# PSUM as one tile of eight single banks: a gated mix of an S4D convolution and a ReLU feed-forward

## The chip, the cores and the metric

The kernel runs on one core of one Trainium2 chip. Its time is the device time of one execution in microseconds; lower is better. The time before is the median of three runs. A profile is one execution of its own, and its span goes from the first to the last instruction.

## The reference

Everything is fp32. With `u` of 2048 positions by 640 channels (N = 128 states, a hidden width of 1728), shortened:

```python
g  = sigmoid((u * gate_w).sum(-1, keepdims=True))
dt = exp(log_dt); A = -exp(log_A_real) + 1j*A_imag; C = (C_real + 1j*C_imag) * dt[:, None]
K  = 2 * einsum("dn,dnl->dl", C, exp((A*dt[:, None])[:, :, None] * pos)).real   # 640 x 2048
a  = causal_conv(K, u) + u * D_skip          # through an FFT of length 4096 in the reference
b  = relu(u @ w1) @ w2
out = g * a + (1 - g) * b
```

## The kernel before

Three kinds of work share the engines.

*Feed-forward.* Each fp32 operand is split into a high and a low fp32r part, and a product is three matmuls (high-high, high-low, low-high). The 1728 hidden columns are 14 blocks, worked off in three passes (`PARTS`, 5, 5 and 4 blocks), each over all eight groups of 256 positions. `hidden` and `wide` make the hidden layer, `sums` multiplies by w2; the sum of a pass goes through DRAM to the next. ScalarE (ACT) makes the high part from PSUM, VectorE (DVE) the low part. All its accumulators are the PSUM tile `pf`, a pool of two single banks.

*Generation of K* (`products`, `factors`, `taps`): TensorE (PE) makes phases and exponents into a four-bank tile `pg`, ACT takes exp and sin, DVE multiplies, and PE sums over the states into `pk` (one bank, also used to transpose `u`). K goes to DRAM (`kd`). Together with `pe` (one bank) these three fill the other six banks until K is done.

*Convolution* (`conv`), in five tiles of 128 channels, as a transform in two stages, a complex product, and the same back. A tile's buffer is `ku`, two of which exist. Its steps, with the names of their task queues:

- stage 1 (`sk` for K, `su` for u): four tasks each, a 64-point transform by the table `tf`; DVE transposes the result in blocks of 32 by 32 from PSUM into `ku`, two instructions a task. `load_u` fetches u for one tile into `xu`.
- stage 2 (`s2`): eight groups j; PE multiplies by `tm`. PSUM then holds the transforms of K and of u. ACT copies that of K to `ku`, DVE makes the two kinds of products into `ku` and `kx`, GpSimd (POOL) adds and subtracts.
- inverse stage 2 (`inv2`, table `tn`), halves h = 0 and 1, each needing the POOL results of its four groups; ACT copies back to `ku`.
- relay (`rl`): eight DVE transposes; then inverse stage 1 (`inv1`, queue `s4`, table `tw`), ACT multiplies by the gate, POOL adds the feed-forward's part sum, and the result leaves through SyncE (SP) queues.

All PSUM of the convolution is the tile `pc`, a pool of three, each of two banks. Every step there works on both banks at once: one ACT copy reads 512 elements a partition from two half banks, and a u transpose reads 16 columns of both.

The order of all work is written out: each piece is a task in a queue, and a string `ORDER` (one letter a task, a number before it repeats) says which queue's next task is issued. This sets each engine's own order, and engines then wait for each other by semaphores alone. PE's queue mixes feed-forward blocks between those of the other two kinds. All instructions are recorded through one helper, so a row of the profile has the helper's line, L186 (L185 in the changed kernel), and tiles tell the steps apart.

A row of PE's order counts an fp32 matmul once, while the profile records it twice: the order's `tm ... x16` (one group of stage 2) is the profile's x32. Feed-forward matmuls are fp32r and are recorded once.

Of the kernel before, what the change touches and what calls it, by code (L numbers as in the profile page):

```python
# [26 lines left out]
LATE = 4  # L27
KX = 3
# [7 lines left out]
YJ = 2  # L36
# [83 lines left out]
class Token:  # L120


    def __init__(self, ring):
        self.ring, self.left = ring, 0


class Ring:
    def __init__(self, n):
        self.free = n
# [6 lines left out]
class Plan:  # L136
# [25 lines left out]
    def run(self):  # L162
        queues = {k: iter(self.queues.pop(tuple(x.split('.')))) for k, x in QUEUES.items()}
        assert not self.queues, list(self.queues)
        for n, k in re.findall(r'(\d*)(\D)', ORDER):
            for _ in range(int(n or 1)):
                t = next(queues[k])
                assert all(d.done for d in t.deps), (k, n)
                for b in t.take:
                    b.ring.free -= 1  # L170
                    assert b.ring.free >= 0, (k, n)
                t.fn()
                t.done = True
                for b in (*t.take, *t.use):
                    b.left -= 1
                    b.ring.free += b.left == 0
# [30 lines left out]
class Kernel:  # L207
    def __init__(self, tc, ctx, io, out):
# [20 lines left out]
        self.pb = ctx.enter_context(tc.tile_pool(name="psf", bufs=2, space=PSUM))  # L229
# [7 lines left out]
    def feed_forward(self):  # L237
# [3 lines left out]
        pa, pb = self.pa, self.pb  # L241
        for n, k in dict(ws=3, wq=5, wo=2, xs=XS, xhl=2, q=2, bank=2, z=1).items():
            ring(n, k)
# [92 lines left out]
        def trans(g, third, src):  # L336
            s_, ld = src
            bank = ('pk', 'pe', 'pg')[0 if g else third]
            b_ = tok(bank)
# [5 lines left out]
            def pe():  # L345
                ps = self.psg.tile([128, 8 if bank == 'pg' else 2, 256], F32, name=bank)
                ps = st['xb', g, third] = ps[:, :2]
# [13 lines left out]
            a = A('PE', 'ff', pe, [ld], take=[b_], use=[s_])  # L361
# [31 lines left out]
        def hidden(p, g, i, fs):  # L393
            b_, h_ = tok('bank'), tok(f"h{i}")

            def pe(r, f, third):
                def go():
                    if r == third == 0:
                        st['hb'] = st['hb', i] = pb.tile([128, 2, 256], F32, name="pf")
# [56 lines left out]
        def wide(p, P, f):  # L456
            ring_ = ("h0", "h2")[f] if f < 2 else f"hw{f}" if p == 1 else ("w14", "w24")[f - 2]
            b_, h_, xs_ = tok('bank'), tok(ring_), [xtok[p, 2 * P + i] for i in range(2)]
# [37 lines left out]
        def sums(p, g, j, q_, qld):  # L496
# [8 lines left out]
            b_ = tok('bank')  # L505
# [7 lines left out]
            def pe(ks):  # L513
                def go():
                    if ks[0] == 0:
                        st['sb', g, j] = pb.tile([128, 320], F32, name="pf")
# [85 lines left out]
        def spin():  # L602
            p = self.psg.tile([128, 2, 256], F32, name="pe").rearrange("p a b -> p (a b)")
            for _ in range(SPIN):
                self.E.matmul(p[:, :128], self.ident, self.ident, start=True, stop=True)
        if SPIN:
            A('PE', 'ff', spin)
# [3 lines left out]
        def spread_gate():  # L611
            p = st['gb'] = self.psg.tile([128, 8, 256], F32, name="pg").rearrange("p a b -> p (a b)")[:, :D]
# [99 lines left out]
        self.last_wide = done[1, 1],  # L712
        for x, gs in self.need_sums:
# [140 lines left out]
    def ssm(self, C=16):  # L854
# [8 lines left out]
        self.c_ps, self.psg = self.cm_enter(name="psg", bufs=1, space=PSUM)  # L863
# [492 lines left out]
```

## Time and profile before

| | us |
|---|---|
| runs | 620.28, 621.45, 622.0; median 621.45 |
| profiled execution | 621.33 |
| its span | 619.5 (1.8 less than its own time) |
| PE busy | 605.9 (98%) |
| DVE busy | 505.9 (82%) |
| ACT busy | 376.1 (61%) |
| POOL busy | 83.9 (14%) |

Rows read: engine, operation, output tile, input tiles, shapes, count; then busy time and the mean of one in ns; then the engine's idle time ahead of them and what ended it. In a timeline a row is start, length, and the merged instructions, with an idle time in brackets. The matmuls overlap in the array, so a length is longer than the step from one start to the next; it is the steps between starts that add up to time.

### The profile page before, as it was taken

The page shows a single profiled execution, that of the slowest core. Times are in us where ns is not written, and L with a number is a line of the kernel's source. Part 1 is how long each engine was busy: PE and PEld are TensorE (multiplying, and loading weights), DVE is VectorE, ACT ScalarE, POOL GpSimd, SP SyncE. Part 2 cuts the span into 40 slices and gives each one's busy share as a digit, 9 for nine tenths or more (in the row PEclk, how much of TensorE's full clock was granted, in tenths as well). Part 3 has the DMA queues.
Part 4 walks back from the last instruction along what each step waited for, and adds up shares of the span by engine and source line. Part 5 has one row for each costly group of instructions (what it writes and reads, how often), then busy time and mean ns, then how long its engine had stood idle before and what let it go on. Part 6 is the DMA issues. An engine that isn't in the chain of part 4 may idle for free.

```text
span 619.5 us, 19956 instructions
## 1 busy us (share of the span) xinstructions
PE 605.9 (98%) x8676; PEld 492.8 (80%) x8676; DVE 505.9 (82%) x841; ACT 376.1 (61%) x539; POOL 83.9 (14%) x114
## 2 busy tenths in 40 slices
PE   7999999999999999999999999999999999999997
PEld 6999998889987898898898888676646755667666
DVE  3798966899999999999999966887859768968642
ACT  3654438999999998899989821313351453432561
POOL 0000000000000000000000000024250360731735
PEclk8999999999999999999999999999999999999999
DMA  9783666135246535453643338982526766664276
GB/s 232 199 321 93 213 218 221 42 81 163 82 134 216 189 138 185 162 170 82 212 165 137 111 116 259 280 247 84 110 75 226 179 156 197 151 168 158 67 200 184
DMA packets 75457, 102.56 MB, mean 166 GB/s; under 512 B 7529, under 2 KB 58601, under 8 KB 75114
## 3 DMA queue, kind: packets, MB, share of 16 engines
q1 hardware_dynamic: 74970, 100.39, 53.8%
q8 instruction: 68, 1.11, 0.8%
q10 hardware_dynamic: 400, 0.90, 0.5%
q14 instruction: 19, 0.16, 0.1%
HBM read 62.21 MB, written 39.06 MB: 163 GB/s over the span
## 4 chain that ended last, share of the span: by engine, by line
PE 76%; ACT 8%; DVE 7%; DMA 4%; issue 2%; SPq 1%; POOL 1%; ACTq 0%; DVEq 0%; POOLq 0%
PE pf L186 51%; PE pc L186 15%; PE pk L186 6%; PE pg L186 4%; ACT sc L186 4%; DVE ku L186 3%; ACT L186 2%; SPq L186 1%; ACT mg L186 1%; DMA xu<-in_A_u_dram 1%; DMA ck<-kd 1%; DVE sc L186 1%; DVE mg L186 1%; DVE G L186 1%; DMA out_dram<-yo 1%
## 5 line engine op out<-in xcount | busy, mean ns | idle before, releaser
L186 PE MATMUL pf<-xx,w1h 128*128 128x256 f32 (+1 forms) x760 | 187.0, 344 | 0.0
L186 PEld LDWEIGHTS pf<-xx,w1h 128*128 128x128 f32 x760 | 124.9, 192 | 28.0 <-issue 13.4
L186 POOL TENSOR_TENSOR ku<-ku,kx 128x256 f32<-128x256 f32 x80 | 56.7, 738 | 473.5 <-DVE ku L186 438.3
L186 PE MATMUL pf<-xx,w1l 128*128 128x512 f32 (+1 forms) x340 | 115.9, 341 | 0.0
L186 ACT COPY ku<-pc 128x512 f32<-128x512 f32 (+1 forms) x60 | 43.7, 753 | 100.4 <-PE pc L186 89.1
L186 PE MATMUL pf<-w2h,hh 128*128 128x320 f32 x288 | 91.4, 322 | 0.3 <-DVE q L186 0.3
L186 DVE STREAM_TRANSPOSE ku<-pc 128x512 f32<-128x512 f32 x80 | 76.8, 1063 | 17.3 <-PE pc L186 17.3
L186 PE MATMUL pf<-w2l,hh 128*128 128x320 f32 x288 | 87.7, 308 | 0.0
L186 PE MATMUL pf<-w2h,hl 128*128 128x320 f32 x256 | 73.7, 313 | 0.0
L186 PEld LDWEIGHTS pf<-xx,w1l 128*128 128x128 f32 x340 | 64.9, 191 | 7.5
L186 PEld LDWEIGHTS pf<-w2h,hh 128*128 128x128 f32 x288 | 54.0, 188 | 11.1 <-issue 5.3
L186 ACT ACT_TABLE_LOAD x42 | 53.9, 1283 | 1.7 <-DVE sc L186 1.0
L186 PEld LDWEIGHTS pf<-w2l,hh 128*128 128x128 f32 x288 | 54.1, 188 | 0.2
L186 DVE TENSOR_TENSOR mg<-mg,sc 128x1024 f32<-128x1024 f32 x40 | 49.0, 1224 | 3.5 <-DVE G L186 0.5
L186 ACT COPY sc<-pg 128x1024 f32<-128x1024 f32 x40 | 40.4, 1010 | 14.7 <-PE pg L186 14.6
L186 DVE TENSOR_TENSOR sc<-sc,mg 128x1024 f32<-128x1024 f32 x40 | 48.6, 1216 | 0.0
L186 PEld LDWEIGHTS pf<-w2h,hl 128*128 128x128 f32 x256 | 46.4, 188 | 2.0 <-issue 1.2
L186 ACT ACTIVATE sc<-sc,half_pi 128x1024 f32<-128x1024 f32 x40 | 45.6, 1140 | 0.0
L186 ACT ACTIVATE hh<-pf 128x512 fp32r<-128x512 f32 (+1 forms) x40 | 20.4, 510 | 36.5 <-PE pf L186 36.5
L186 ACT ACTIVATE sc<-sc 128x1024 f32<-128x1024 f32 x40 | 42.2, 1054 | 0.2
L186 ACT ACTIVATE mg<-pg 128x1024 f32<-128x1024 f32 x40 | 41.7, 1043 | 0.2
L186 PE MATMUL pc<-ku,tm 64*32 64x256 f32 x1280 | 39.8, 379 | 0.6 <-DVE ku L186 0.5
(171 smaller groups left out, 1127.3 us busy)
## 6 DMA issues: line engine op xcount, KB each, us to landing
xx<-xt SPq DMA_DIRECT2D x24, 640.0 KB, 6.5
xt<-xx SPq DMA_DIRECT2D x16, 640.0 KB, 5.0
part<-q SPq DMA_DIRECT2D x16, 640.0 KB, 4.7
q<-part SPq DMA_DIRECT2D x16, 640.0 KB, 4.6
ws<-in_B_w_dram SPq DMA_DIRECT2D x20, 320.0 KB, 3.4
kd<-kt SPq DMA_DIRECT2D x80, 64.0 KB, 3.1
ck<-kd SPq DMA_DIRECT2D x40, 128.0 KB, 3.4
xu<-in_A_u_dram SPq DMA_DIRECT2D x10, 512.0 KB, 8.4
```

The source lines that it names most:

```text
L186: return lambda *a, **k: self._tc.keep_in_program_order(f(*a, **k))
```

## The change

One PSUM tile `ps` of 128 x 8 x 512 fp32 replaces the pools `pf`, `pg`, `pk`, `pe` and `pc`. A ring `bk` of eight hands out single banks, first freed first taken, to all three kinds of work. Four of the eight are held for `pg` (banks 0 to 3) until K is done, so that feed-forward, taps and input transposes share four in that time and everything shares eight afterwards.

In the convolution each instruction now touches one bank. Stage 1 and inverse stage 1 take two single banks, stage 2 two, inverse stage 2 four. `load_u` fetches halves of the channels: a partition half holds 32 positions by 64 channels (runs of 256 bytes in DRAM) where it held 16 by 128 (runs of 512 bytes), so that a transpose of u reads one bank. In stage 2 ACT makes two copies of 256 elements a group where it made one of 512; DVE still makes two products of 512 elements, but one a bank, both into `kx`; POOL takes both operands from `kx`. The ACT copies back after inverse stage 2 are four of 512 elements where there were two of 1024. `kx` has two buffers of twice the size where it had three. The part sums that are added at the end of a tile lie in `xu` behind u, in one buffer where there were two. Buffers of the convolution open later (`room`): after the last sums of the second pass, where they opened when K was done. And `ORDER` is another one throughout.

The numbers of matmuls, DVE products, transposes and POOL additions are the same; ACT has 60 copies more.

```diff
 class Ring:
     def __init__(self, n):
-        self.free = n
+        self.free = list(range(n))
...
                 for b in t.take:
-                    b.ring.free -= 1
-                    assert b.ring.free >= 0, (k, n)
+                    b.slot = b.ring.free.pop(0)
...
+        self.hold = [tok('bk') for _ in range(4)]
+        self.prm0 = A('PY', 'open', lambda: None, take=self.hold)
...
-        opened = self.opened = A('PY', 'open', start, [self.kd_out])
+        opened = A('PY', 'open', lambda: None, [self.kd_out], use=self.hold)
+        room = self.room = A('PY', 'open', start, [opened])
...
+        self.room.deps += done[1, 0].deps + done[1, 1].deps
...
-                    D_.dma_start(t[64 * h:64 * h + 64], ud[:, 16 * h:16 * h + 16, i * C:i * C + C])
+                    D_.dma_start(t[64 * h:64 * h + 64], ud[:, :, i * C + h * H:i * C + h * H + H])
...
         def stage2(i, j, dep):
-            b_, x_ = tok('psc'), tok('kx')
+            bs, x_ = [tok('bk') for _ in range(2)], tok('kx')
...
-                            self.E.matmul(ps[32 * m:32 * m + 32, p, 2 * a:2 * a + 2], st['tm'][r, g, 32 * a:32 * a + 32],
-                                          st['ku', i][r, :, g], start=True, stop=True)
+                            self.E.matmul(self.ps[32 * m:32 * m + 32, bs[p].slot, 256 * a:256 * a + 256],
+                                          st['tm'][r, g, 32 * a:32 * a + 32], st['ku', i][r, :, g], start=True, stop=True)
...
-            def copy():
-                S.copy(whole(i, j), st['p2', i, j][:, 0])
+            def copy(p):
+                return lambda: S.copy(halves(p), parts(p)[:, 0])
...
-                    V.tensor_mul(st['kx', i, j] if a else k, st['p2', i, j][:, 1, None, a].to_broadcast([128, 2, 2, C]), k)
+                    V.tensor_mul(st['kx', i, j][:, p], parts(p)[:, 1, :, None].to_broadcast([128, 2, 2, C]),
+                                 halves(p)[:, None].to_broadcast([128, 2, 2, C]))
...
-                    y, x = whole(i, j)[:, k], st['kx', i, j][:, 1 - k]
-                    (P.tensor_add if k else P.tensor_sub)(y, y, x)
+                    x = st['kx', i, j]
+                    (P.tensor_add if k else P.tensor_sub)(whole(i, j)[:, k], x[:, :, 0, k], x[:, :, 1, 1 - k])
...
-            bs = tok('psc'), tok('psc')
+            bs = [tok('bk') for _ in range(4)]
```

PE's order at the second tile's stage 2. `pf` are feed-forward matmuls; `pc<-ku,tm` is stage 2 (x16 is one group), `tw` inverse stage 1 of the tile before, `tn` half an inverse stage 2. Before:

```order
L186 MATMUL pc<-ku,tm 32x256 x48
L186 MATMUL pf<-xx,w1h_5364 128x512 x2
L186 MATMUL pf<-xx,w1l_5365 128x512
L186 MATMUL pc<-ku,tm 32x256 x16
L186 MATMUL pf<-xx,w1h_5364 128x512 x2
L186 MATMUL pf<-xx,w1l_5365 128x512
L186 MATMUL pc<-ku,tm 32x256 x32
L186 MATMUL pf<-xx,w1h_5364 128x512 x2
L186 MATMUL pf<-xx,w1l_5365 128x512
L186 MATMUL pc<-ku,tm 32x256 x32
L186 MATMUL pc<-ku,tw 64x512 x8
```

The same place in the changed kernel, from the end of the feed-forward stretch that parts the tile's two runs of four groups:

```order
L185 MATMUL ps<-xx,w1h_4974 128x512 x2
L185 MATMUL ps<-xx,w1l_4975 128x512
L185 MATMUL ps<-ku,tm 32x256 x64
L185 MATMUL ps<-ku,tw 64x512 x8
L185 MATMUL ps<-ku,tn 64x128 x64
L185 MATMUL ps<-ck,tf 64x512 x8
L185 MATMUL ps<-xx,w1h_5197 128x512 x2
```

Short feed-forward pieces between groups are gone; the eight groups are two runs of four, and the second is followed by three other steps of the convolution at once. Counted over all of PE's order from the first stage 1 on, feed-forward stands between convolution blocks in 26 places where it stood in 44, and the blocks of one kind of convolution matmul (`tf`, `tm`, `tn`, `tw`) number 49 where they numbered 58. Runs of up to five groups of stage 2 occur (twice).

DVE's order at the third tile's stage 2 (`ku<-ku` are relay transposes of the tile before, `ku<-pc` or `ku<-ps` with 128x16x32 the transposes of stage 1, `q` and `hl` feed-forward). Before:

```order
L186 SCALAR_TENSOR_TENSOR q<-pf,omg,q 128x320
L186 TENSOR_TENSOR kx<-pc,ku 128x512
L186 STREAM_TRANSPOSE ku<-ku 128x8x2x32 x2
L186 TENSOR_TENSOR ku<-pc,ku 128x512
L186 TENSOR_TENSOR kx<-pc,ku 128x512
L186 SCALAR_TENSOR_TENSOR q<-pf,omg,q 128x320
L186 TENSOR_TENSOR ku<-pc,ku 128x512
L186 STREAM_TRANSPOSE ku<-ku 128x8x2x32 x2
L186 TENSOR_TENSOR kx<-pc,ku 128x512
L186 STREAM_TRANSPOSE ku<-ku 128x8x2x32
L186 TENSOR_TENSOR ku<-pc,ku 128x512
```

In the changed kernel:

```order
L185 STREAM_TRANSPOSE ku<-ku 128x8x2x32
L185 TENSOR_TENSOR kx<-ps,ku 128x512 x6
L185 STREAM_TRANSPOSE ku<-ku 128x8x2x32 x2
L185 TENSOR_TENSOR kx<-ps,ku 128x512 x4
L185 SCALAR_TENSOR_TENSOR hl_6829<-ps,hh_6828 128x512
L185 TENSOR_TENSOR kx<-ps,ku 128x512 x6
L185 STREAM_TRANSPOSE ku<-ps 128x16x32 x16
```

Products of three groups (six), two and three stand together, where other work stood between nearly all of the first four.

PE's order at the very start (`ident` alone are warm-up matmuls, `ident,xu` the transposes of the first input, `gw,ones` the spread of the gate's weights). Before:

```order
L186 MATMUL pe<-ident 128x128 x10
L186 MATMUL pk<-ident,xu 128x128 x4
L186 MATMUL pe<-ident,xu 128x128 x4
L186 MATMUL pg<-ident,xu 128x128 x2
L186 MATMUL pg<-gw,ones 128x512
```

And now:

```order
L185 MATMUL ps<-ident 128x128 x10
L185 MATMUL ps<-ident,xu 128x128 x8
L185 MATMUL ps<-gw,ones 128x512
L185 MATMUL ps<-gw,ones 128x128
L185 MATMUL ps<-ident,xu 128x128 x2
```

The gate's matmul stands ahead of the last transposes and in banks of its own. On SP the first input now goes ahead of the first weights, which went first; on ACT the split of those first weights goes ahead of the splits of the input, which went first.

More of the change, by code (lines that the diff above doesn't have):

```diff
@@ L175, in run @@
                     b.left -= 1
-                    b.ring.free += b.left == 0
+                    if b.left == 0:
+                        b.ring.free.append(b.slot)
         assert not any(next(q, None) for q in queues.values())
@@ L337, in trans @@
             s_, ld = src
-            bank = ('pk', 'pe', 'pg')[0 if g else third]
-            b_ = tok(bank)
+            b_ = tok('bk')
             if third == 0:
@@ L345, in pe @@
             def pe():
-                ps = self.psg.tile([128, 8 if bank == 'pg' else 2, 256], F32, name=bank)
-                ps = st['xb', g, third] = ps[:, :2]
+                ps = st['xb', g, third] = self.ps[:, b_.slot].rearrange("p (k t) -> p k t", t=256)
                 for k in range(kn):
@@ L393, in hidden @@
         def hidden(p, g, i, fs):
-            b_, h_ = tok('bank'), tok(f"h{i}")
+            b_, h_ = tok('bk'), tok(f"h{i}")
             def pe(r, f, third):
@@ L601, in feed_forward, with spin @@
         self.zs, self.x_read = [], []
-        def spin():
-            p = self.psg.tile([128, 2, 256], F32, name="pe").rearrange("p a b -> p (a b)")
+        b_ = tok('bk')
+        def spin(b_=b_):
             for _ in range(SPIN):
-                self.E.matmul(p[:, :128], self.ident, self.ident, start=True, stop=True)
+                self.E.matmul(self.ps[:, b_.slot, :128], self.ident, self.ident, start=True, stop=True)
         if SPIN:
-            A('PE', 'ff', spin)
+            A('PE', 'ff', spin, [self.prm0], take=[b_])
         def load_gate():
@@ L1128, in stage1 @@
             new = k and q == 0
-            a = A('PE', 's' + kind, pe, [ld, tf, opened] + ([] if k else [first[i]]), take=[b_, buf] if new else [b_], use=[s_] if new else [s_, buf])
-            pes[kind, i, q] = a
-            ts = [A('DVE', 's' + kind, turn(h), [a], use=[b_, buf])
-                  for h in range(2)]
+            a = A('PE', 's' + kind, pe, [ld, tf, opened] + ([] if k else [first[i]]), take=[*bs, buf] if new else bs,
+                  use=[s_] if new else [s_, buf])
+            ts = [A('DVE', 's' + kind, turn(h), [a, room] if k else [a], use=[bs[h], buf]) for h in range(2)]
             if new:
@@ L1163, in go @@
                 def go():
-                    y, x = whole(i, j)[:, k], st['kx', i, j][:, 1 - k]
-                    (P.tensor_add if k else P.tensor_sub)(y, y, x)
-                return go
-            f = A('PE', None, pe, dep, take=[b_], use=[K[i]])
-            c = [A('ACT', 's2', copy, [f], use=[b_, K[i]])]
-            for a in (1, 0):
-                c.append(A('DVE', 's2', mul(a), c, take=[x_] if a else (), use=[b_, K[i]] + [x_] * (1 - a)))
+                    x = st['kx', i, j]
+                    (P.tensor_add if k else P.tensor_sub)(whole(i, j)[:, k], x[:, :, 0, k], x[:, :, 1, 1 - k])
+                return go
+            f = A('PE', None, pe, dep, take=bs, use=[K[i]])
+            c = [A('ACT', 's2', copy(p), [f], use=[bs[p], K[i]]) for p in range(2)]
+            c = [A('DVE', 's2', mul(p), [c[p]], take=() if p else [x_], use=[bs[p], K[i]] + [x_] * p) for p in range(2)]
+            used.setdefault(i, []).append(f)
             return f, [A('POOL', 's2', add(k), c, use=[x_, K[i]]) for k in range(2)]
@@ L1201, in inv2 @@
                 vs.append(A('PE', None, lambda gs=gs: pe(gs), [*dep, tn] + vs[-1:], take=() if t else bs,
-                            use=[K[i]] + (list(bs) if t else [])))
+                            use=[K[i]] + (bs if t else [])))
             v = vs[-1]
-            return vs, [A('ACT', 's2', back(k), [v], use=[bs[k], K[i]]) for k in range(2)]
+            return vs, [A('ACT', 's3', back(m), [v, *used[i]], use=[bs[m], K[i]]) for m in range(4)]
         def relay(i, r, dep):
@@ L1241, in copy @@
                         o = self.gy[:, b0 + b] if last and b >= ns else st['yo', i, b0][:, b]
-                        S.mul(o, st['p4', i, j][:, q, b], self.gate[:, b0 + b:b0 + b + 1])
+                        S.mul(o, st['p4', i, j, q][:, b], self.gate[:, b0 + b:b0 + b + 1])
                 c = A('ACT', 's4', copy, [a], take=[x for x in (y_, g_ if first else None) if x],
-                      use=[b_] + ([g_] if g_ and not first else []))
+                      use=[bs[q]] + ([g_] if g_ and not first else []))
                 self.need_gates.append(c)
@@ L1278, in out @@
                             stq.dma_start(od[h, :, b0:b0 + ns, i * C:i * C + C], st['yo', i, b0][64 * h:64 * h + 64, :ns])
-                    ld = A('SP', 'yq', load, [opened], take=[j_] if new else (), use=() if new else [j_])
+                    ld = A('SP', 'yq', load, [opened, self.u_first], take=[j_] if new else (), use=() if new else [j_])
                     self.need_sums.append((ld, [(b0 + b) // 2 for b in range(0, ns, 2)]))
```

147 lines of the change are left out of this document (67 added, 80 removed), and 16 rows, old and new, of the table QUEUES.

## The prediction

> **What bounds the kernel now.** I read the page's busy line and the shares of the chain that ended last, then the busy time by stage (windows: length, then busy time and instructions of each engine, PE's clock, DMA), then PE's timeline inside the convolution.
>
> ```profile
> span 619.5 us, 19956 instructions
> ...
> PE 605.9 (98%) x8676; PEld 492.8 (80%) x8676; DVE 505.9 (82%) x841; ACT 376.1 (61%) x539; POOL 83.9 (14%) x114
> ...
> PE 76%; ACT 8%; DVE 7%; DMA 4%; issue 2%; SPq 1%; POOL 1%; ACTq 0%; DVEq 0%; POOLq 0%
> ```
>
> ```profile
> core 0: us, PE busy (x) PEld busy (x) DVE busy (x) ACT busy (x) POOL busy (x), PEclk, DMA share, GB/s
> 0.00:17.00 17.00, 12.72 (x72) 11.69 (x73) 5.84 (x15) 6.96 (x13) 0.88 (x7) 0.90 0.91 247
> 17.00:94.00 77.00, 76.30 (x586) 75.48 (x585) 64.24 (x138) 37.26 (x78) 0.00 (x0) 1.00 0.64 205
> 94.00:365.00 271.00, 268.35 (x4362) 236.72 (x4361) 255.13 (x432) 243.26 (x273) 0.00 (x0) 1.00 0.45 144
> 365.00:600.00 235.00, 233.22 (x3567) 155.25 (x3567) 176.35 (x251) 84.47 (x162) 72.33 (x96) 1.00 0.60 169
> 600.00:619.50 19.50, 15.30 (x100) 13.67 (x96) 4.32 (x8) 4.09 (x16) 10.66 (x11) 1.00 0.69 190
> ```
>
> The profiled execution took 621.33 us, 1.8 more than its span, and 0.1 less than the median, 621.45; the sum is made against it. PE is the bound in every stage. It is idle 4.3 us at the start (17.00 - 12.72), 0.7 in the first feed-forward stretch, 2.7 while K is generated (DVE 94% and ACT 90% busy beside it), 1.8 in the convolution (365 to 600) and 4.2 at the end. Since the matmuls are the same before and after, a gain has to come out of the 4.3, or out of time that counts as busy and is not work. That second kind is visible at the edges between kinds of matmul. This is PE in stage 2 of the second tile:
>
> ```profile
> 440.65 0.39 PE L186 MATMUL pf<-xx,w1l 128*128 128x512 f32 x1
> 440.88 0.61 PE L186 MATMUL pf<-xx,w1h 128*128 128x512 f32 x2
> 441.33 0.39 PE L186 MATMUL pf<-xx,w1l 128*128 128x512 f32 x1
> 441.65 2.82 PE L186 MATMUL pc<-ku,tm 64*32 64x256 f32 x96
> 444.40 0.73 PE L186 MATMUL pf<-xx,w1h 128*128 128x512 f32 x2
> 444.98 0.39 PE L186 MATMUL pf<-xx,w1l 128*128 128x512 f32 x1
> 445.29 1.09 PE L186 MATMUL pc<-ku,tm 64*32 64x256 f32 x32
> 446.32 0.73 PE L186 MATMUL pf<-xx,w1h 128*128 128x512 f32 x2
> 446.89 0.40 PE L186 MATMUL pf<-xx,w1l 128*128 128x512 f32 x1
> 447.21 1.96 PE L186 MATMUL pc<-ku,tm 64*32 64x256 f32 x64
> 449.10 0.73 PE L186 MATMUL pf<-xx,w1h 128*128 128x512 f32 x2
> ```
>
> From start to start. Inside a feed-forward stretch a 512-wide matmul takes 0.227 us (440.65 to 441.33 are three). Three of them between two stage 2 blocks take 0.89 (444.40 to 445.29, and 446.32 to 447.21), so the interruption costs 0.89 - 0.68 = 0.21 beyond its work. Blocks of one, two and three groups take 1.03 (445.29 to 446.32), 1.89 (447.21 to 449.10) and 2.75 (441.65 to 444.40): 0.86 a group and 0.17 a block. No idle time stands in these rows; the edges are counted as busy.
>
> **The change part by part.**
>
> *Edges in the convolution.* By the two orders, feed-forward interrupts the convolution 26 times instead of 44, and the blocks of one kind number 49 instead of 58. At the prices above: 18 x 0.21 = 3.8, and 9 x 0.17 = 1.5 less; together -5.3. The block price is measured on stage 2, which loses 6 blocks; stage 1 loses 4 and the first inverse step gains 1, and for these it is taken over. If only the edge out of feed-forward counted (441.65 - 441.33 - 0.23 = 0.09) and blocks cost nothing, the term would be 18 x 0.09 = 1.6; its ends are -1.6 and -5.3, and I take the latter because whole interruptions were measured twice at 0.21.
>
> *Waits that longer runs bring.* A group of stage 2 fills two banks, and a bank is free when its ACT copy and its DVE product are done.
>
> ```profile
> L186 ACT COPY ku<-pc 128x512 f32<-128x512 f32 x40 | 23.6, 590 | 51.7 <-PE pc L186 40.4 <-issue 11.1
> L186 ACT COPY ku<-pc 128x1024 f32<-128x1024 f32 x20 | 20.4, 1079 | 48.7 <-PE pc L186 48.7
> L186 ACT CAST xx<-pg 128x256 fp32r<-128x256 f32 x1 | 0.4, 390 | 0.0
> L186 DVE TENSOR_TENSOR kx<-pc,ku 128x512 f32<-128x512 f32 x40 | 27.2, 680 | 4.8 <-ACT ku L186 4.3 <-POOL ku L186 0.6
> L186 DVE TENSOR_TENSOR ku<-pc,ku 128x512 f32<-128x512 f32 x40 | 27.2, 681 | 0.9
> L186 DVE STREAM_TRANSPOSE ku<-pc 128x512 f32<-128x512 f32 x80 | 76.8, 1063 | 17.3 <-PE pc L186 17.3
> L186 POOL TENSOR_TENSOR ku<-ku,kx 128x256 f32<-128x256 f32 x80 | 56.7, 738 | 473.5 <-DVE ku L186 438.3 <-PE pc L186 34.9
> ```
>
> DVE needs 2 x 0.68 = 1.36 us a group, PE 0.86. Of a run of five, the fifth needs the two banks of the first (the fourth one of them, if an unfinished feed-forward sum holds a bank). With the nearest row for a 256-wide copy, 0.39, the first group's banks are free 0.39 + 1.36 = 1.75 us after PE ends it; PE gets to the fifth 3 x 0.86 = 2.6 after that. So a run of five fits, with 0.8 us to spare, if DVE is free. By the order two runs have five groups and two have four. I take 0.3 us for each of five, since DVE has other work between, and 0.2 in the first tile, where the second half of inverse stage 2 follows only four short blocks behind the last group and needs that group's products (1.36) and POOL results (2 x 0.74). Taken: +0.8. Below, the 1.8 us of idle time in this stage could go too (-1.8); above, see the first rival (+10).
>
> *ACT.* 80 copies of 0.39 for 40 of 0.59, and 40 of 0.59 for 20 of 1.08: 31.2 + 23.6 - 23.6 - 21.6 = +9.6 us, in a stage where ACT is busy 84 of 235 us. Nothing on PE; per group the first DVE product can start 0.2 us sooner. If this cover were gone it would show as DVE waiting for `ku` copies. POOL's 80 additions and DVE's 80 products keep their shapes: 0.
>
> *The start.*
>
> ```profile
> 0.73 0.46 SPq L186 DMA_DIRECT2D wq<-in_B_w_dram  x1
> 1.25 0.59 SPq L186 DMA_DIRECT2D xu<-in_A_u_dram  x1
> 6.73 0.66 PE L186 MATMUL pk<-ident,xu 128*128 128x128 f32 x4 [1.11 <-DMA xu<-in_A_u_dram]
> 8.04 0.69 DVE L186 TENSOR_TENSOR xx<-pk,xx 128x512 fp32r<-128x512 f32 x1 [6.87 <-ACT xx L186]
> 8.65 0.68 DVE L186 TENSOR_TENSOR xx<-pe,xx 128x512 fp32r<-128x512 f32 x1
> 8.65 1.73 ACT L186 CAST w1h<-wq 128x320 fp32r<-128x320 f32 x3
> 9.72 1.34 PE L186 MATMUL pg<-gw,ones 1*128 1x512 f32 x4 [1.68 <-DVE xx L186]
> 10.99 2.32 PE L186 MATMUL pf<-xx,w1h 128*128 128x256 f32 x12
> ```
>
> Three things move. The input is issued 0.5 us sooner on SP (1.25 - 0.73) and PE waits for it at 6.73. The gate's matmul (1.3 us) waited 1.7 for DVE to leave `pg`; it now has banks of its own and stands ahead of the last transposes, so the feed-forward, which followed it at 10.99, waits only for DVE's low parts of the input (ended at 9.33, now 0.5 sooner) and of the first weights (some 0.5 more): near 9.9 with the releases. Against it, ACT now splits the first weights ahead of the input; they are issued 0.5 later, and had landed by 8.65 at the latest (no wait stands there). At best -1.2; if they land only at 9.2, ACT's three input splits end some 1.8 late. I take -0.7, since the input, twice as large and issued next, took 5.5 us (1.25 to 6.73), so the weights should be in by the time the transposes end; and the rest of the gain may be given back in the 0.7 us of waits that follow.
>
> *The u loads.* Runs of 256 bytes for 512, so twice the pieces.
>
> ```profile
> xu<-in_A_u_dram SPq DMA_DIRECT2D x10, 512.0 KB, 8.4
> 383.04 1.39 SPq L186 DMA_DIRECT2D xu<-in_A_u_dram  x2
> 397.19 1.04 PE L186 MATMUL pc<-xu,tf 64*64 64x512 f32 x8
> ```
>
> The first tile's u has 14.1 us from issue to use; in the new order one stage 1 block fewer (0.9) stands between, so 13.2, over the 8.4 it takes. Other tiles have more. At the same time for a byte it costs nothing; at the same time for a piece, 16.8, it would be 3.6 late. Cost 0 taken, ends 0 and +3.6. The Trainium skill (DMA: Bandwidth & Descriptors, Specifications) sets 512 B as the smallest transfer at line rate, which the old load met and the new one does not: by that rule the late end is the nearer one and the sum would be 3.6 higher. No row here times such pieces alone.
>
> *Feed-forward moved ahead.* In the new order the last taps stand 12 feed-forward steps later, so about 8 us of that work (a step is three 512-wide or five 320-wide matmuls, near 0.7) leaves the convolution, where 153 steps cover its chains instead of 165. PE's work is the same and the price is 0 as long as the chains are shorter than PE's own work there; the cover that is left is 1.8 us of idle time against 233 of work. If they are not, up to 8 us come back as idle time (second rival).
>
> *Other moves.* The tables of the convolution (`tm`, `tn`) are issued later, after the second pass, with some 20 feed-forward steps ahead of the first stage 2: hidden. One buffer of part sums for two: POOL waits, off PE. In generation the order has 28 edges from feed-forward to `pg` instead of 29: 0.2, left out. The end is the same last feed-forward group, eviction and store: 0.
>
> Sum: -5.3 + 0.8 - 0.7 = -5.2, from 621.33: 616.1. I say 616.2.
>
> **The rivals.**
>
> *Slower: DVE decides.* PSUM is then emptied too late for the longer runs. DVE may be behind when a run starts: it executes sixteen stage 1 transposes (17 us at 1.06) and eight relay transposes ahead of the products of some runs. With d us of delay, the fifth group of a run (or the fourth, with a bank held) waits d - 0.8. At d = 3.3 on the four long runs PE waits 4 x 2.5 = 10 us, and 621.33 - 6.0 + 10 = 625. It decides from d near 2.3 on (4 x 1.5 eats the gain of 6.0). For it: DVE is 75% busy in this stage (176 of 235) and has to fit the same work in 230. Against it: DVE waits for PE 17.3 us in total ahead of its stage 1 transposes, so it is not the one that is late as a rule. The Trainium skill (TensorEngine Tiling (Array Packing), PSUM Bottleneck) warns of just this: tiling speeds up TensorE and not the emptying of PSUM, which may become the bottleneck; the trace shows the ratio (1.36 against 0.86 a group) and not yet the wait.
>
> *No change: the edges come back as idle time.* PE's stretch 365 to 600 shortens only if ACT, DVE, POOL and the u load finish their chains sooner; a late first u (+3.6), or chains that keep their length under less cover (+5 of the 8), leave PE idle where it had edges: 620 to 622. For it: the chain that ended last leaves PE for ACT, DVE and DMA in 19% of the span.
>
> *More gained.* The idle 1.8 us of the convolution and the 2.7 of generation go too, with more banks to run ahead into, and the start gives 1.2: 621.33 - 5.3 - 1.2 - 3 = 611.8.
>
> That the change does not do what it says is no rival: the orders show single-bank instructions and the fewer edges.
>
> **How the numbers follow.** A difference under 0.3% (1.9 us) cannot be told from no change. Forecast (613.5 to 619.5): 0.50. More gained: 0.13. No change (619.6 to 623.3): 0.19. DVE decides: 0.18. Faster 0.63, same 0.19, slower 0.18. The range, 612 to 623, takes in the forecast, no change and nearly all of the case of more gained; it leaves out the case in which DVE decides and little else. The forecast's own range is 613.5 to 619.5.
>
> **What would show it.** Right: fewer and longer `tm` blocks at 0.86 a group and 0.17 a block, the convolution from the first stage 1 to the last `tw` some 13 us shorter (8 of feed-forward moved out of it, 5 of edges), PE idle there still near 2 us, the first feed-forward matmul near 10. Wrong: PE idle ahead of `tm` or `tn` released by DVE or ACT in several us; PE idle ahead of the first `xu,tf` for DMA; the first feed-forward matmul after 11.

## The result, and the profile after

| | runs | median, us | ratio to before (95% interval) |
|---|---|---|---|
| before, measured again beside it | 619.59 to 622.0 | 620.87 | |
| after | 610.44 to 612.05 | 611.38 | 0.9847 (0.9821 to 0.9873) |

The change made the kernel 9.5 us faster, where 5.2 were forecast: the direction was right, and the time lies 0.6 us below the low end of the range. The profiled execution took 611.85 us. Its page, the lines that answer to those shown of before:

```profile
span 610.1 us, 20050 instructions
...
PE 598.8 (98%) x8676; PEld 496.4 (81%) x8676; DVE 504.8 (83%) x841; ACT 379.7 (62%) x599; POOL 83.9 (14%) x114
...
PE 91%; DMA 3%; SPq 2%; POOL 1%; ACT 1%; issue 1%; DVE 0%; POOLq 0%; ACTq 0%
```

PE has the same matmuls and is busy 7.1 us less, so most of the gain was time that counts as busy. The chain that ended last now runs through PE for 91% of the span (76% before), and ACT and DVE are nearly gone from it. By stage (length, then busy time and instructions of each engine, PE's clock, DMA):

```profile
core 0: us, PE busy (x) PEld busy (x) DVE busy (x) ACT busy (x) POOL busy (x), PEclk, DMA share, GB/s
0.00:17.00 17.00, 12.28 (x71) 10.96 (x72) 6.99 (x17) 8.93 (x17) 0.87 (x7) 0.95 0.93 243
17.00:94.00 77.00, 77.00 (x591) 76.63 (x594) 61.76 (x131) 34.93 (x75) 0.00 (x0) 0.99 0.66 208
94.00:365.00 271.00, 269.92 (x4278) 240.91 (x4274) 255.71 (x430) 243.58 (x273) 0.00 (x0) 1.00 0.45 146
365.00:600.00 235.00, 234.63 (x3712) 163.16 (x3712) 178.18 (x261) 90.31 (x233) 77.98 (x101) 1.00 0.66 174
600.00:610.10 10.10, 4.98 (x34) 4.72 (x33) 2.11 (x4) 1.92 (x4) 5.08 (x7) 0.96 0.63 186
```

PE's idle time fell from 2.7 to 1.1 us in generation and from 1.8 to 0.4 in the convolution's window. To see the rest, I took the *lost time* of each stage from both traces: the steps from start to start of PE's matmuls, less the steps that the same matmuls have inside an undisturbed run (0.227 us for a 512-wide feed-forward matmul, 0.1465 for a 320-wide one). It holds the edges, the short waits and the low clock together. Generation begins with the first `pg` matmul, the convolution with the first stage 1, and ends with the last `tw`.

| lost time, us | before | after | difference |
|---|---|---|---|
| start, to the first `pg` | 9.1 | 8.6 | -0.5 |
| generation | 18.3 | 14.7 | -3.7 |
| convolution | 15.7 | 9.8 | -5.9 |
| feed-forward at the end | 0.7 | 0.1 | -0.6 |
| from the start of PE's last matmul to the end of the span | 4.2 | 5.4 | +1.2 |

The rows add up to -9.5, which is the difference of the two spans before rounding. The convolution lost 5.9 less, where edges and waits together were forecast at 4.5 (5.3 less 0.8); generation, which the prediction left out, gave 3.7.

In the convolution kinds now follow each other with no feed-forward between. This is PE at the place whose order is shown above: the second run of stage 2 of the second tile (`tm`), inverse stage 1 of the first tile (`tw`), inverse stage 2 of the second (`tn`) and stage 1 of the third (`tf`):

```profile
442.82 3.68 PE L185 MATMUL ps<-ku,tm 64*32 64x256 f32 x128
446.43 3.66 PE L185 MATMUL ps<-ku,tw 128*64 128x512 f32 x16
450.02 2.10 PE L185 MATMUL ps<-ku,tn 32*64 32x128 f32 x128
452.05 2.24 PE L185 MATMUL ps<-ck,tf 64*64 64x512 f32 x16
454.21 0.73 PE L185 MATMUL ps<-xx,w1h 128*128 128x512 f32 x2
```

Four groups of stage 2 take 3.61 us (446.43 - 442.82), which is 4 x 0.86 + 0.17 as in the rows of before: the group and block prices held, and no row has an idle time in brackets. The engines behind PE:

```profile
L185 DVE STREAM_TRANSPOSE ku<-ps 128x512 f32<-128x512 f32 x80 | 75.7, 1057 | 11.5 <-PE ps L185 11.4
L185 DVE TENSOR_TENSOR kx<-ps,ku 128x512 f32<-128x512 f32 x80 | 50.6, 681 | 14.0 <-ACT ku L185 8.3 <-POOL ku L185 4.3 <-issue 1.0
L185 ACT COPY ku<-ps 128x256 f32<-128x256 f32 x80 | 26.2, 385 | 35.5 <-PE ps L185 35.1
xu<-in_A_u_dram SPq DMA_DIRECT2D x10, 512.0 KB, 8.2
```

DVE still waits for PE 11.4 us ahead of its transposes, so it does not decide. The ACT copy of 256 columns takes 0.385 us (0.39 was taken), and the u load in runs of 256 bytes lands in 8.2 us where runs of 512 took 8.4.

### The profile page after: what moved, and what is told of

Same layout as the page of the kernel before. It is cut to its first block, busy times and chain, and to the rows that moved or that the text cites. A ratio compares the mean times of both kernels' runs of the same rounds, so it can differ in the third digit from the quotient of the medians.

```text
span 610.1 us, 20050 instructions
## 1 busy us (share of the span) xinstructions
PE 598.8 (98%) x8676; PEld 496.4 (81%) x8676; DVE 504.8 (83%) x841; ACT 379.7 (62%) x599; POOL 83.9 (14%) x114
## 4 chain that ended last, share of the span: by engine, by line
PE 91%; DMA 3%; SPq 2%; POOL 1%; ACT 1%; issue 1%; DVE 0%; POOLq 0%; ACTq 0%
PE ps L185 91%; SPq L185 2%; DMA xu<-in_A_u_dram 1%; DMA out_dram<-yo 1%; POOL yo L185 1%; POOL q L185 1%; DMA xu<-part 1%; ACT yo L185 0%; ACT L185 0%; ACT mg L185 0%; ACT ku L185 0%; ACT q L185 0%; DVE q L185 0%; POOLq L1344 0%; ACTq L185 0%
## 5 line engine op out<-in xcount | busy, mean ns | idle before, releaser
L185 PE MATMUL ps<-xx,w1h 128*128 128x256 f32 (+1 forms) x760 | 185.3, 341 | 0.5 <-ACT xx L185 0.5
L185 PEld LDWEIGHTS ps<-xx,w1h 128*128 128x128 f32 x760 | 125.9, 191 | 22.5 <-issue 4.2
L185 POOL TENSOR_TENSOR ku<-kx 128x256 f32<-128x256 f32 x80 | 56.7, 738 | 462.5 <-DMA xu<-in_A_u_dram 408.4
L185 PE MATMUL ps<-xx,w1l 128*128 128x512 f32 (+1 forms) x340 | 116.2, 342 | 0.0
L185 PE MATMUL ps<-w2h,hh 128*128 128x320 f32 x288 | 91.2, 320 | 0.0
L185 PE MATMUL ps<-w2l,hh 128*128 128x320 f32 x288 | 87.7, 308 | 0.4 <-issue 0.4
L185 DVE STREAM_TRANSPOSE ku<-ps 128x512 f32<-128x512 f32 x80 | 75.7, 1057 | 11.5 <-PE ps L185 11.4
L185 PE MATMUL ps<-w2h,hl 128*128 128x320 f32 x256 | 73.1, 311 | 0.0
L185 PEld LDWEIGHTS ps<-xx,w1l 128*128 128x128 f32 x340 | 65.0, 191 | 7.4
L185 PEld LDWEIGHTS ps<-w2h,hh 128*128 128x128 f32 x288 | 54.1, 188 | 8.4 <-DVE ku L185 2.8
```

What stands on the lines that cost most here:

```text
L185: return lambda *a, **k: self._tc.keep_in_program_order(f(*a, **k))
```

## The experiments

Each is compared with the kernel before on the same chip, whose medians there were 621.83 to 622.62 us. The kernel after was not run again beside them, and before is 1.0 to 1.7 us slower here than in the first table (620.87), so a difference to after of less than 2 us is not clear; lost times within the traces compare better. Two theories stood at the start: A, the new order made the gain; B, the banks did. All edits are on the kernel after.

**The old order on the new form.** `ORDER` is that of the kernel before.

```
-ORDER = ('!PD;T4;mD;Da;Fan; ...
+ORDER = (the string of before, its tasks under the new letters)
```

> The changed kernel (one PSUM tile, single banks, halves of channels) with the order of the kernel before, in which only what the new form forbids is moved (two transposes of K wait for the buffers, some part sums and products for theirs; PE's order is the old one but for one step at the start). Lost time of a stage is its length less PE's matmuls at the steps they have inside an undisturbed run (0.227 us for a 512-wide feed-forward matmul). Before it was 18.3 us in generation and 15.7 in the convolution, after 14.7 and 9.8. Theory A, the new order made the gain: generation stays near 18 and the convolution near 15.5, 620 us in all. Theory B, the banks made it (eight of them, handed out one by one, so that PE finds one free whatever the order): generation falls to 15, and the convolution loses its waits but keeps the 17 interruptions at some 0.37, 13 to 14; 615 us.

Measured: 629.62 us, 1.0109 (1.0083 to 1.0136): 1.1% slower than before. Generation lost 17.6, as theory A said. But the convolution lost 22.8, which neither had. One place explains it. POOL, DVE and PE at the third tile, a fence for each:

```profile
499.62 1.27 POOL L185 TENSOR_TENSOR yo<-yo,xu 128x512 f32<-128x512 f32 x1 [4.81 <-ACT yo L185]
504.91 1.26 POOL L185 TENSOR_TENSOR yo<-yo,xu 128x512 f32<-128x512 f32 x1 [4.03 <-DMA xu<-part]
506.13 4.22 POOL L185 TENSOR_TENSOR ku<-kx 128x256 f32<-128x256 f32 x6
```

```profile
507.56 1.29 DVE L185 TENSOR_TENSOR kx<-ps,ku 128x512 f32<-128x512 f32 x2 [11.44 <-POOL ku L185]
```

```profile
503.32 1.93 PE L185 MATMUL ps<-ck,tf 64*64 64x512 f32 x10
508.31 1.98 PE L185 MATMUL ps<-ck,tf 64*64 64x512 f32 x6 [3.06 <-DVE kx L185]
```

Read from the bottom: PE stands in the middle of stage 1, because a bank still holds stage 2 results; DVE cannot take them, because both `kx` buffers wait for POOL; POOL adds part sums, and waits 4.03 us for the second ones, which could be fetched only when the one buffer `xu` was free. "POOL waits, off PE" was the prediction's sentence on that buffer. In the order of after it is true; in the order of before it is not.

**The same with two buffers of part sums.**

```
-ck=2, cu=1, kx=KX, yo=2, yj=1, K=2
+ck=2, cu=1, kx=KX, yo=2, yj=2, K=2
-st['yj', i, b0] = self.xu[:, 16 * C:]...
+st['yj', i, b0] = self.pr.tile([128, 4, C], F32, name="yj", bufs=1) if j_.slot else self.xu[:, 16 * C:]...
```

> The kernel of the run before with the old order (changed kernel, old order, 629.6 us), with a second buffer for the part sums that are added at the end of a tile, as the kernel before had. In its trace POOL waits 4.0 us at 500.9 for part sums that could be fetched only when the first buffer was free, POOL's products of stage 2 stand behind that, DVE waits 11.4 us for `kx`, and PE loses 8.6 us from 488 to 510. Theory D, that one place is what the new form costs under the old order: 621 us, the lost time of the convolution back at 14 to 16. Rival, the single banks themselves cost (PE asks for a bank that is not the one freed first): 626 or more, with waits of PE for banks at many places.

Measured: 616.83, 0.9922 (0.9907 to 0.9937). In this kernel the two sums of a pair could still land in one buffer, so its time is no measure of two buffers, and it was made again with `def load(b0=b0, ns=ns, j_=j_)`, which gives each load its own:

> The run before with two buffers of part sums gave 616.8 us, but there some sums of a pair went to the same buffer, so that its output was not the reference's; here each load goes to its own. Theory D (the one buffer is what the new form costs under the old order): 617, lost time 17.6 in generation and 14.5 in the convolution as in that run; the new form alone is then 5 us faster than the kernel before, and the new order another 5.5. If the shared buffer hid waits: 619 to 622.

Measured: 615.88, 0.9892 (0.9861 to 0.9923), 13.7 less than with one buffer. Lost time: start 7.2, generation 17.6, convolution 12.8. The one buffer was the loss of the old order on the new form, most of it at that place (the same nine blocks of PE, from the `tm` block at 488.6 us on, lost 10.4 us there and 1.8 here), and the rival (waits at many places) is out. And the new form alone, with the old order and this buffer, is 6.7 us faster than before on that chip: of its lost time 1.9 went at the start, 0.7 in generation, 2.9 in the convolution and 0.6 at the end. From there to after, the new order takes 2.9 more in generation and 3.0 in the convolution, while the start lost 1.4 more in after. Where the convolution's lost time went, by kind of matmul (blocks that end inside the stage, so one interruption fewer than in the prediction's count; `tw` is -0.5 in all three):

| us (blocks) | feed-forward | stage 1, `tf` | `tm` | `tn` |
|---|---|---|---|---|
| before | 9.2 (43) | 0.6 (21) | 2.6 (19) | 3.9 (11) |
| new form, old order, two sums | 9.0 (43) | 0.3 (21) | 1.2 (19) | 2.8 (11) |
| after | 5.3 (25) | 2.0 (17) | 1.1 (13) | 1.9 (12) |

The form, at the same blocks, takes away short waits ahead of and inside `tm` and `tn`, 2.7 us in all. The order takes the 18 interruptions (3.7) and 0.9 of `tn`, and brings 1.7 of waits inside stage 1; `tm` loses six blocks and stays, so waits of nearly their price seem to have come in there. That all of these are waits for banks is likely and not shown: no row of PE names them.

**The old order in the start and generation alone.**

```
-ORDER = (new order)
+ORDER = (old order up to the first stage 1, then what is left in the new order)
```

> The changed kernel with the old order up to the first stage 1 and the new order from there (the 12 feed-forward steps that the new order has ahead of the last taps stand between). Theory A (order): generation loses 17.6 as with the old order throughout, the convolution 9.8 as after; 611.4 + 2.9 = 614.3, less some 1.5 by the old start, 613. Theory B (banks): generation stays at 14.7, 610 to 611.

Measured: 612.68, 0.9858 (0.9838 to 0.9878). Lost time: start 7.3, generation 17.8, convolution 9.7, as theory A said. The two parts of the order act independently, and the new order in generation is worth 3. PE's waits for ACT ahead of `pg` (94 to 365 us) are 2.2 us here, 1.1 in after (1.3 in before). By the medians this version is only 1.3 us slower than after, since the start lost 1.3 less: in these executions no gain of the new order at the start is seen.

**More interruptions.** One feed-forward step is moved between two groups of stage 2, 17 times; for instance in PE's order of the first tile, 10 steps, 3 groups, 4 steps, 3 groups become 9, 1, 1, 1, 1, 1, ... .

```
 ORDER, PE's letters alone (D feed-forward, H group of stage 2):
-10D 3H 4D 3H 5D 2H
+9D H D H D H 2D H D H D H 3D H D H
```

> The changed kernel with 17 more interruptions in the convolution: 17 times a single feed-forward step is moved between two groups of stage 2 that stood side by side (43 interruptions instead of 26; before had 44). Nothing else is moved but what must follow. By the prices of the prediction, 0.21 an interruption and 0.17 a block, it loses 17 x 0.38 = 6.5 us: 617.9. If an interruption costs only the step out of feed-forward (0.09): 1.5, 612.9. If runs of groups make PE wait for DVE, which single steps between them relieve, the loss is smaller than 6.5 by those waits, down to 4.

Measured: 617.11, 0.9916 (0.9895 to 0.9938), 5.7 more than after by the medians; the lost time of the convolution rose from 9.8 to 17.2, and the start was 1.3 shorter in this execution (its clock, below). Feed-forward rose by 3.5 (17 x 0.205), `tm` by 3.0 (17 x 0.177): the prediction's 0.21 and 0.17, each confirmed. PE there:

```profile
410.62 0.31 PE L185 MATMUL ps<-w2h,w2l 128*128 128x320 f32 x1
410.86 1.09 PE L185 MATMUL ps<-ku,tm 64*32 64x256 f32 x32
411.89 0.41 PE L185 MATMUL ps<-w2h,hh 128*128 128x320 f32 x1
412.14 0.31 PE L185 MATMUL ps<-w2l,hh 128*128 128x320 f32 x1
412.28 0.31 PE L185 MATMUL ps<-w2h,hl 128*128 128x320 f32 x1
```

The interruption's 0.2 has two halves: the step out of feed-forward is 0.24 (410.86 - 410.62) and the first one after a block 0.25 (412.14 - 411.89), where the next is 0.14. Only the first half stood in the prediction's low end.

**Which bank comes next.**

```
-self.free = list(range(n))
+self.free = list(range(n))[::-1]
-b.slot = b.ring.free.pop(0)
+b.slot = b.ring.free.pop()
```

> The changed kernel in its own order, but the bank that was freed last is taken first, so that PE asks for a bank soon after its last reader was issued instead of as late as possible. Theory A (order): what counts is how many banks there are and what stands between, and the time stays at 611.4, within 1. Theory B (banks handed out oldest first give the slack): the short waits come back, 2 us or more in generation and as much in the convolution, 615 us or more, seen as stops of 0.1 to 0.5 us ahead of taps, products and feed-forward.

Measured: 639.8, 1.0268 (1.024 to 1.0296), 28 us above after, with every engine's order unchanged. Generation lost 22.6, the convolution 29.7. Theory B's direction, far beyond its size. What PE waited for from 380 us on:

```profile
engine line waited for: us in total, times, longest us
PE ps L185 <- DVE ku L185: 6.9, 11, 1.2
PE ps L185 <- ACT yo L185: 3.3, 5, 1.2
PE ps L185 <- DVE kx L185: 2.8, 7, 0.4
...
```

These are the readers of banks. The Trainium skill (Perfetto Trace Analysis, Optimizing Tensor Performance) asks to rotate independent groups through different banks; the runs agree, and add that with eight banks in use, the rotation's direction alone is worth 28 us here.

**How many banks feed-forward has in generation.** A feed-forward sum is open from its first matmul's start until its last reader on ACT or DVE has ended. By the traces before never has more than two open. After has three or four open in 87 of the 278 us of generation. The two runs above with the old order in generation on the new form, whose feed-forward could take four banks as well, never have more than two for any time that shows, and there generation lost 17.6 (with two buffers of part sums) and 17.8, nearly as before. So it is the order that opens more. The first try to forbid that:

```
 ORDER rewritten: a third block waits until an older one is emptied; other tasks go ahead
```

> The changed kernel in its own order, but while K is generated no feed-forward block is begun while two others are not yet emptied, as the two banks of the kernel before enforced; the new order has three or four open at 128 of its 367 rows of PE there. Products and taps keep their place among ACT's and DVE's work. Theory E, the third and fourth bank are what the new order gains by in generation: lost time there back from 14.7 to 17.5, 614.2 us. Rival, the gain lies in where products and taps stand and not in how many blocks are open: 611.4, within 0.8.

Measured: 627.67, 1.009 (1.0064 to 1.0117); generation lost 30.5. Both theories missed, since the edit did more than meant: `pg` products went ahead of the steps that were held back, and PE waited 11.6 us for ACT to empty the one set of `pg` banks. It tells nothing of banks, and three or four sums were still open in 55 us of it. The second try leaves every engine's own order alone and changes only which bank is taken (the string is written anew so that banks are returned in time, with the same sequence for each engine):

```
+own = [x for x in b.ring.free if x in b.own and not conv]
+b.slot = (own or b.ring.free)[0]
+b.ring.free.remove(b.slot)
 feed-forward tokens: own = 4, 5; taps and input transposes: own = 6, 7
```

> The changed kernel with every engine's order unchanged; only which bank a task gets is changed, until the convolution starts: feed-forward takes banks 4 and 5 alone, taps and input transposes 6 and 7 (2 of 104 takings in generation find theirs taken and use another), as in the kernel before. Theory E (the third and fourth bank for feed-forward are what the new order's gain in generation rests on): lost time in generation from 14.7 to 18 or more, 615 us or more. Rival (the places of products and taps in the order give it): 14.7 as after, 611 to 612.

Measured: 699.43, 1.123 (1.1195 to 1.1264), 88 us above after, all of it in generation, which lost 102. PE's waits from 91 to 456 us, and that window:

```profile
engine line waited for: us in total, times, longest us
PE ps L188 <- DVE hl L188: 22.0, 6, 6.7
PE ps L188 <- DVE q L188: 21.7, 8, 4.3
PE ps L188 <- ACT q L188: 12.1, 7, 3.6
...
```

```profile
91.00:456.00 365.00, 306.48 (x4433) 267.54 (x4433) 261.85 (x438) 244.58 (x274) 0.00 (x0) 0.91 0.34 112
```

PE waits 56 us for feed-forward's own readers: the order puts products of K ahead of them on ACT and DVE, and the third and fourth block are what PE does meanwhile (here a third is open in only 18 us). The granted clock was 0.91 in that window, which can explain much of the other 30 us. So theories A and B are one: this order cannot be had without the shared banks, and the banks without the order give only a part. What no run separates is whether the open sums themselves take away the 3 us, or the places of products and taps that go with them.

**The start.** In after PE does not wait for the gate any more, reaches the second group's input early and waits there:

```profile
7.52 1.34 PE L185 MATMUL ps<-gw,ones 1*128 1x512 f32 x4
8.79 0.44 PE L185 MATMUL ps<-ident,xu 128*128 128x128 f32 x2
9.73 1.67 PE L185 MATMUL ps<-xx,w1h 128*128 128x256 f32 x12 [0.50 <-ACT xx L185]
11.24 0.33 PE L185 MATMUL ps<-xx,w1l 128*128 128x256 f32 x1
...
14.91 0.67 PE L185 MATMUL ps<-ident,xu 128*128 128x128 f32 x4 [1.92 <-DMA xu<-in_A_u_dram]
15.30 0.72 PE L185 MATMUL ps<-xx,w1h 128*128 128x256 f32 x2
15.81 0.42 PE L185 MATMUL ps<-xx,w1l 128*128 128x256 f32 x1
16.03 0.63 PE L185 MATMUL ps<-xx,w1h 128*128 128x256 f32 x2
```

Moving those transposes behind the second step of the hidden layer:

```
-for third in range(k_, 3 if i + 2 >= n else k_ + 1):
+for third in range(k_, 3 if i + 2 >= n else k_ + 1) if g else ((), (0,), (1, 2))[k_]:
```

> The changed kernel with the transposes of the second group of inputs one step of the hidden layer later (after the second instead of after the first, their last two thirds after the third). In the profile after, PE comes to them at 12.8 us and waits 1.9 us for the load; then its granted clock is 0.5 to 0.7 from 15 to 19 us, and a feed-forward triple takes 0.64 us instead of 0.36. Theory C, the wait brings the low clock: both go, 1.9 + 1.6 = 3.5 us less, 607.9. Rival, the low clock comes at that time whatever PE did: 1.9 less, 609.5. Second rival, another wait takes the place (the splits of the next weights, which DVE ended at 13.7): 1 us or less, 610.4 or more.

Measured: 610.66, 0.9815 (0.9789 to 0.9841), 0.7 less than after. The wait of 1.9 is gone, but the clock was low from 8.8 to 12.2 us instead, under the first feed-forward matmuls:

```profile
9.80 2.73 PE L185 MATMUL ps<-xx,w1h 128*128 128x256 f32 x12
12.36 0.28 PE L185 MATMUL ps<-xx,w1l 128*128 128x256 f32 x1
```

Twelve matmuls take 2.56 us here and 1.51 in after (11.24 - 9.73). With two more empty matmuls at the start (`SPIN = 12`), so that PE is not idle ahead of the first input:

> The kernel with the later second input (610.7 us) with 12 instead of 10 empty matmuls at the start, so that PE is busy from 1.5 to 6.5 us, until the first input is there; its wait there was 0.9 us, and its granted clock was 0.5 from 8.8 to 12.2 us, 3.4 us in which the twelve first feed-forward matmuls took 2.56 instead of 1.51. Theory C (PE's idle time brings the low clock): no low clock up to 24 us, 1.3 less, 609.4. Rival, it comes anyhow, since it also came and went with no relation to the longest wait (none at all in the run with the 17 interruptions, after a wait of 2.1): 610.7, with a stretch of 0.5 somewhere in the first 24 us.

Measured: 610.37, 0.9818 (0.98 to 0.9835). The profiled execution has no low clock in its first 28 us, and the start lost 5.8 where it had 7.4; the median moved by only 0.3, less than the spread of its runs (609.98 to 611.24). Theory C is favoured and not settled: the run with more interruptions had no low clock either, after a wait of 2.1 us.

**Three buffers for the results.**

```
-YO = 2
+YO = 3
```

> The fastest so far (later second input, 12 empty matmuls, 610.4) with three buffers for a tile's results instead of two. In the profile after, ACT waits 21.9 us in all for results to leave their buffer, and PE's rows have three weight loads that wait 1.5 us in all for ACT's results. Theory F (that is what stops PE inside stage 1 blocks, some 2 us): 608.5. Rival: PE's waits are for other banks, and nothing changes: 610.4.

Measured: 609.5, 0.9792 (0.9759 to 0.9824), the fastest version. The waits inside stage 1 fell by 0.9 (from 2.0 in after to 1.0), and those inside `tm` rose as much, so the stated reason did not hold: the convolution lost 9.8 as in after. The interval overlaps those of the two versions before it and of after; that the three edits together, 1.9 us by the medians, beat after is likely and not proved.

## Why the prediction was right or wrong

- *Edges in the convolution, -5.3.* Right. Eighteen interruptions gave 3.7 (3.8 forecast), at prices that 17 interruptions put back confirmed. The block term (-1.5) holds for stage 2 (0.177 a block, six fewer, 1.0); for stage 1 it was taken over, and nothing in the table shows it.
- *Waits that longer runs bring, +0.8.* The wrong sign. Waits inside stage 1 came (+1.7), some in `tm`, and PE was stopped by no DVE row; but the form took away 2.7 of short waits in `tm`, `tn` and stage 1 at unchanged blocks. The lower end (-1.8 of visible idle time) named this; the upper end was taken too seriously.
- *Generation, "0.2, left out".* The step that failed: it gave -3.7. The prediction counted edges there, found 29 and 28, and stopped. It looked for time that counts as busy and is not work only at edges, and did not ask how many feed-forward sums are open at once, though it named the eight shared banks. With the new order three or four are open for 87 us where before had two, and short waits go in the taps, the input transposes and at the edge from feed-forward to `pg`; 1.6 of it is idle time in the windows, the rest lies in rows that count as busy. That the order does it is shown (3.1 of it comes back with the old order there); how each short wait goes is inferred.
- *The start, -0.7.* -0.5 measured. The first feed-forward matmul came at 9.73 (near 10 forecast), 1.26 sooner, and most of the gain was given back at a wait that the prediction did not see: the second group's input. With the old order at the start the new form lost only 7.2 to 7.3 there, so the gate's own bank can have given all of it.
- *The u loads, 0.* Right. The smaller runs landed as fast (8.2 against 8.4 us), and no wait of PE for u stands in the rows. The rule of the Trainium skill (DMA: Bandwidth & Descriptors, Specifications) that would have cost 3.6 did not show here.
- *Feed-forward moved ahead, 0; ACT, 0.* Right: the convolution from the first stage 1 to the last `tw` is 14.0 us shorter (13 forecast), with 0.4 us of idle time.
- *The one buffer of part sums, "POOL waits, off PE".* Right only with the new order; with the old one it costs 13.7 us.
- *The end, 0.* +0.6: feed-forward lost 0.6 less, and the last stores ended 1.2 later. That tail was between 4.2 and 6.2 us in the executions profiled, so no cause is claimed.

Sum as measured: -4.7 for interruptions and stage 2's blocks, -1.2 for waits in the convolution, -3.7 in generation, -0.5 at the start, +0.6 at the end: -9.5 with these roundings. Of the rivals, "more gained" is what happened, at 611.8 against 611.4, and the mechanism it named (more banks to run ahead into) is the one that the runs favour. That the total is so near is partly luck: its 1.2 at the start were 0.5, and its 2.7 of generation, all idle time, were 3.7, mostly not idle time. The range began at 612 and so left out this rival's own figure, though the prediction says that it takes in nearly all of that case. "DVE decides" did not come near.

## What to carry to other kernels

When storage is pooled, count how many pieces are open at once under each order, not only how often kinds alternate: a stage whose edges look alike can still gain by running further ahead, and short waits hide in rows that the profile counts as busy. An order and its buffers are one thing: the old order on the new form with one buffer of part sums, the new order on the old partition, and the new order with another rotation were 8, 77 and 18 us slower than before. After removing a wait at the start, look what the freed engine meets next.

## What the runs showed of the hardware

- PE's granted clock fell to 0.5 for 3.4 us somewhere in the first 19 us (for 6.8 in one run) in nine of the thirteen kernels profiled. Its rows in after:

```profile
14.00:15.00 1.00, 0.09 (x1) 0.12 (x2) 0.75 (x2) 0.19 (x2) 0.00 (x0) 1.00 1.05 246
15.00:16.00 1.00, 1.00 (x7) 1.00 (x8) 0.63 (x2) 0.70 (x2) 0.00 (x0) 0.69 1.01 374
16.00:17.00 1.00, 1.00 (x7) 1.00 (x6) 0.75 (x2) 1.00 (x3) 0.00 (x0) 0.50 1.04 394
```

  PE's longest idle time ahead of it, after the 1.5 us at the very start, was 1.9 us in after and only 0.4 in the first try to keep two sums open, and once a wait of 2.1 us had no low clock behind it. It cost 1.0 us in one run (2.56 - 1.51) and 1.4 in after (five triples of feed-forward at 0.64 for 0.36), which blurs every comparison of starts. The Trainium skill (TensorE: Matmul & The Clock Gate, Part 1) has a free-running window of some 3.4 us; the lengths here agree with it. These rows add that PE had not been idle for a whole such window ahead of the low clock.
- A block of stage 2 matmuls (fp32) slows the feed-forward beside it twice: 0.09 us on the last matmul ahead of it and 0.11 on the first behind it.
